# Attention scores as four 64x64 products at a time, two steps a visit, in a fused attention and MoE kernel

## The chip, the cores and the metric

The kernel runs on one core of one Trainium2 chip. The time is the device time of one execution in microseconds (us). Before the change the median of three runs is 390.88 us (390.87 to 391.03).

## The reference

```python
# q, k, v: (4 batches, 8 heads, 576 positions, 64 wide)
scores = q @ k^T / 8 - slope[h] * |rel|;  masked to 0 <= rel < 128
attn   = exp(scores - max) / sum
x      = (attn @ v) as (2304 tokens, 512)
# soft MoE: 8 experts, 4 slots each
logits = x @ phi
slots  = softmax_over_tokens(logits)^T @ x
slots  = relu(slots @ w1[e]) @ w2[e]
y      = softmax_over_slots(logits) @ slots
out    = relu(y @ w_in)^2 @ w_out        # 512 -> 2048 -> 512
```

## The kernel before

Everything is one program, in three stages: attention for 16 units (a unit `u` is a batch and a pair of heads), then the experts (H with w1, O with w2, lines 760 and 904), then the last layer (lines 957 and 1001), which is more than half of the time.

In attention a unit is cut into nine chunks `c` of 64 queries. A chunk needs at most 192 keys (itself and the two chunks before). The two heads share the 128 partitions: partitions 0 to 63 hold the 64 dimensions of the first head, 64 to 127 those of the second. One product per chunk gives the scores of both heads: its stationary side `zq` is a 128x128 block matrix, queries of head 0 in one corner, of head 1 in the other, zeros in the two others; its moving side `kq` is the keys, 128 partitions by 64, 128 or 192 columns. A float32 product is two passes through TensorE (PE), so the trace counts two MATMUL and two LDWEIGHTS per product.

A step `t` is two consecutive chunks: `emit_S` (line 180) does two products into one bank of PSUM (tag "S", three banks). Then, per chunk, `emit_max` on VectorE (DVE, line 193) adds the bias and takes the maximum, `emit_exp` on ScalarE (ACT, line 202) takes the exponential; `emit_sums`, `emit_fold` and `emit_norm` on GpSimd (POOL, lines 207 to 235) normalise; `emit_T` (PE, line 249) transposes; `emit_evac` (ACT line 269, DVE line 273) copies the transposes out; when all chunks of a unit are there, `emit_PV` (PE, line 285) multiplies by v, with weights of 64 columns, two heads on the two halves of the array's columns; `emit_xT` copies out (ACT). After that `emit_X` transposes (line 328), and for each batch `emit_logits` (line 315, weights of 32 columns, four on the array at once), `emit_logr` (line 321) and d0 to d4 keep a running softmax over tokens.

The order on every engine is fixed beforehand by `arrange`, a planner: each operation has an estimated duration, the operations it comes after, a due time and the PSUM banks that it takes; the planner gives out what can start first, by due time where two could. On SP, which issues the DMAs, it interleaves the loads of z and k of a unit (`load_z`, `load_k`, after the scores of the unit three earlier, whose buffer they take), of v (`load_v`, after the PV two earlier) and 38 half loads of 512 KB of expert weights (`load_half_w`, lines 82 and 88). Behind the attention, `load_extra` (line 97) loads five more expert tiles of 1 MB as the attention's buffers come free, then the first two tiles `f` of the last layer's weights and seven more tiles of w2 follow, then the other `f` (lines 70 and 74). A tile `f` is unpacked by POOL (line 813) and DVE (lines 826 to 830) before PE can use it.

Of the kernel before, what the change touches and what calls it, by code (L numbers as in the profile page):

```python
# [7 lines left out]
F32 = mybir.dt.float32  # L8
# [20 lines left out]
def attn_moe_relu2_kernel(ctx: ExitStack, tc: tile.TileContext, z, k, v, phi, w1, w2, w_in, w_out, bias, cst, out):  # L29
# [103 lines left out]
    zq = [zpool.tile([128, NCH, 2, 64], F32, name=f"zq{i}") for i in range(NQ)]  # L133
    kq = [zpool.tile([128, S], F32, name=f"kq{i}") for i in range(NQ)]
# [9 lines left out]
    kt_t, v_t, xT = {}, {}, {}  # L144
# [3 lines left out]
    zq.append(first[:, 0:2 * S].rearrange("p (c a b) -> p c a b", c=NCH, a=2))  # L148
    kq.append(first[:, 2 * S:3 * S])
# [250 lines left out]
    load_z(0, 0, 2)  # L400
    load_k(0, 0, 4, act)
    sp.dma_start(out=tbl[:, 0:192], in_=bias[:, 0:192])
    load_z(0, 2, 4, act)
    load_z(0, 4, 6)
    load_k(0, 4, 9, act)
    load_z(0, 6, 9)
    sp.dma_start(out=cs, in_=cst)
    sp.dma_start(out=tbl[:, 192:384], in_=bias[:, 192:384])
    load_z(1, 0, 3)
    load_k(1, 0, 3)  # L410
    load_z(1, 3)
    load_k(1, 3)
# [3 lines left out]
    load_k(2)  # L416
# [19 lines left out]
    STEP = 1450  # L436
# [5 lines left out]
    fin = {u: (NCH * u + NCH - 1) // 2 for u in range(NU)}  # L442
    alone = (0, 1)
    landed = {0: 0, 1: 900, 2: 2600, 3: 3500, 4: 5000, 6: 6000, 9: 10500}
    steps_of = lambda u: range(NCH * u // 2, fin[u] + 1)
    for u in range(1, NU):
        if u > 2:
            before = [x for y in range(u) if zslot(y) == zslot(u) for x in each(emit_S, *steps_of(y))]
            op(load_z, u, "SP", 1450, before, STEP * fin[u - 1] - 20000, (), 2300)
            op(load_k, u, "SP", 740, before, STEP * fin[u - 1] - 19990, (), 2300)  # L450
        op(load_v, u, "SP", 810, each(emit_PV, u - 2)[:u > 1], STEP * fin[u] - 6000, (), 2300)
    op(load_phi, 0, "SP", 200, (), 9000, (), 2300)
    for j in range(2 * RING):
        late = [u for u in range(NU) if zslot(u) == NQ + j // 2 - (RING - NZ)]
        late = late if j // 2 >= RING - NZ else []
        when = 15000 + 2400 * min(j, 31) + 1700 * max(0, j - 31)
        op(load_half_w, j, "SP", 1260, [x for u in late for x in each(emit_S, *steps_of(u))], when + 1000, at=when)
    for t in range(NS):
# [19 lines left out]
        op(emit_T, t, "PE", 222, each(emit_norm, *two), t0 + 3500, (("T", each(emit_evac, *two[:1 + bool(half)])),), 230)  # L478
        op(emit_evac, (t, 0), "ACT", 52 + 106 * len(full), each(emit_T, t) + free(full), t0 + 4000, (), 135)
        if half:  # L480
            op(emit_evac, (t, 1), "DVE", (0, 208, 342)[sum(x[1] > 1 for x in ch)] + 208 * sum(x[1] == 0 for x in ch), each(emit_T, t) + each(emit_evac, (t, 0)) + free(half), t0 + 4300, (), 120)
    for u in range(NU):
        b, kk = divmod(u, NPAIR)
        t0, odd, late = STEP * fin[u], b % 2, u == NU - 1
        parts = [(t, i) for t in range(NCH * u // 2, fin[u] + 1) for i in range(2) if (emit_evac, (t, i)) in ops]
        old = (each(emit_X, u - 4) + each(emit_logr, (u - 4) // NPAIR)) if 4 <= u < NU - 4 + 2 else []
        op(emit_PV, u, "PE", 1910, each(emit_evac, *parts) + each(load_v, u)[:u > 0], t0 + 5500, (("xa", each(emit_xT, u)), ("T" if late else "B", each(emit_xTb, u))), 190, 9500)
        op(emit_xT, u, "ACT", 477, each(emit_PV, u) + old, t0 + 7400, (), 165)
        op(emit_xTb, u, "DVE" if late else "ACT", 104, each(emit_PV, u) + old, t0 + 7450, (), 165)
# [708 lines left out]
```

## Time and profile before

| | us |
|---|---|
| median of three runs | 390.88 |
| the profiled execution's own time | 391.1 |
| its span, first to last instruction | 389.3 |
| PE busy | 381.8 |
| DVE busy | 274.6 |
| ACT busy | 243.9 |
| POOL busy | 117.4 |

Busy is the union of an engine's instructions in time; a PE that is busy need not work at its peak, since the ends of products are modelled. PEld is PE's loading of weights, which lies beside its products. The granted clock of TensorE is 1.0 of full speed in all 40 slices of the page. The chain that ended last runs through PE for 95% of the span.

### The profile page before, as it was taken

How to read it: one execution, taken by the hardware profiler on the slowest of the kernel's cores; microseconds unless marked ns; L12 is line 12 of the kernel's file. 1: busy time of each engine (PE TensorE's matmuls, PEld its weight loads, DVE VectorE, ACT ScalarE, POOL GpSimd, SP SyncE). 2: the span in 40 equal slices, each digit the busy share in tenths (PEclk: the TensorE clock that was granted, in tenths of full speed). 3: DMA queues.
4: the chain of work that ended last, by engine and by line, in shares of the span. 5: the costliest groups of instructions: out<-in, count | busy, mean ns of one | idle time of the engine just before them, and what ended most of it. 6: DMA issues, size and time to landing. Idle time of an engine off the chain costs nothing.

```text
span 389.3 us, 7986 instructions
## 1 busy us (share of the span) xinstructions
PE 381.8 (98%) x2654; PEld 300.2 (77%) x2654; DVE 274.6 (71%) x819; ACT 243.9 (63%) x728; POOL 117.4 (30%) x289
## 2 busy tenths in 40 slices
PE   8899999999999999999999999999999999999996
PEld 8798788788777346777877887888878888888884
DVE  5676786686775957578687888887767785466455
ACT  4989889789874220497776766766666644334440
POOL 4878678568660132131111102102100000000000
PEclk9999999999999999999999999999999999999999
DMA  7989999999978999998102200000000040012004
GB/s 227 339 257 389 411 400 380 387 340 411 397 266 319 416 427 421 417 422 356 43 2 108 109 2 0 0 2 0 0 3 1 0 164 0 2 52 110 2 1 162
DMA packets 23225, 75.36 MB, mean 194 GB/s; under 512 B 2832, under 2 KB 4624, under 8 KB 21520
## 3 DMA queue, kind: packets, MB, share of 16 engines
q1 hardware_dynamic: 22608, 74.30, 49.7%
q10 hardware_dynamic: 576, 0.56, 0.4%
q8 instruction: 21, 0.34, 0.4%
q14 instruction: 20, 0.16, 0.1%
HBM read 70.13 MB, written 4.72 MB: 192 GB/s over the span
## 4 chain that ended last, share of the span: by engine, by line
PE 95%; DVE 2%; POOL 1%; ACT 1%; DMA 1%; issue 0%; DVEq 0%; POOLq 0%; ACTq 0%
PE acc L1001 50%; PE s L184 11%; PE xa L285 7%; PE tp L249 5%; PE h L957 4%; PE H L760 4%; PE O L904 4%; PE X L328 2%; PE L L315 1%; PE MX L853 1%; DVE psum L1019 1%; PE xb L285 1%; DMA kq<-in_k_dram 1%; PE R L381 1%; POOL p L235 1%; PE L L321 1%
## 5 line engine op out<-in xcount | busy, mean ns | idle before, releaser
L1001 PE MATMUL acc<-whl,arena_gh 128*128 128x512 f32 x864 | 216.5, 394 | 0.0
L1001 PEld LDWEIGHTS acc<-whl,arena_gh 128*128 128x128 f32 x864 | 160.1, 188 | 35.3 <-issue 2.9
L986 DVE TENSOR_TENSOR arena_gh<-hT,arena_gh 128x384 fp32r<-128x384 f32 (+1 forms) x97 | 53.6, 553 | 30.1 <-ACT arena_gh L982 24.3
L202 ACT ACTIVATE p<-p,st 128x192 f32<-128x192 f32 (+1 forms) x144 | 61.4, 429 | 5.8 <-DVE st L193 5.1
L969 ACT ACTIVATE acc<-h 128x384 f32<-128x384 f32 x47 | 23.1, 493 | 64.9 <-PE h L957 64.9
L813 POOL TENSOR_SCALAR yw<-f 128x512 f32<-128x512 f32 x32 | 27.4, 862 | 99.2 <-DVE arena_cin L830 53.5
L235 POOL TENSOR_SCALAR p<-p,st 128x128 f32<-128x128 f32 (+1 forms) x142 | 49.8, 371 | 6.5 <-DVE st L212 5.1
L193 DVE CUSTOM_DVE_ANT_0 p<-s,tbl 128x192 f32<-128x192 f32 (+1 forms) x144 | 41.7, 325 | 10.4 <-PE s L184 10.2
L184 PE MATMUL s<-kq,zq 128*128 128x192 f32 (+2 forms) x198 | 39.3, 328 | 0.3 <-DMA kq<-in_k_dram 0.2
L957 PE MATMUL h<-cst_sb,Mst 128*128 128x384 f32 x95 | 32.2, 339 | 0.1
L184 PEld LDWEIGHTS s<-kq,zq 128*128 128x128 f32 x198 | 31.2, 199 | 1.0 <-DMA kq<-in_k_dram 0.5
L273 DVE TENSOR_SCALAR ptb<-tp 128x256 f32<-128x256 f32 (+1 forms) x64 | 24.1, 384 | 8.0 <-ACT ptb L269 7.8
L269 ACT ACTIVATE ptb<-tp 128x256 f32<-128x256 f32 (+1 forms) x72 | 25.2, 353 | 7.1 <-PE tp L249 6.5
L249 PE MATMUL tp<-cs,p 128*128 128x128 f32 x144 | 28.0, 281 | 1.5 <-POOL p L235 1.4
L227 POOL TENSOR_TENSOR p<-p 128x128 f32<-128x128 f32 (+1 forms) x63 | 26.8, 425 | 7.0 <-ACT p L202 4.3
L285 PE MATMUL xa<-ptb,vt 128*64 128x256 f32 (+1 forms) x256 | 27.8, 359 | 0.0
L202 ACT ACTIVATION_READ_ACCUMULATOR p<-p,st 128x1 f32 x144 | 27.4, 190 | 0.0
L978 DVE TENSOR_TENSOR hT<-acc 128x384 f32<-128x384 f32 x17 | 9.5, 557 | 23.3 <-ACT acc L969 23.2
L982 ACT ACTIVATE arena_gh<-hT 128x384 fp32r<-128x384 f32 x48 | 24.8, 516 | 0.7
L285 PEld LDWEIGHTS xa<-ptb,vt 128*64 128x64 f32 x256 | 16.9, 136 | 10.0 <-issue 2.8
L982 ACT ACTIVATE arena_gh<-acc 128x384 fp32r<-128x384 f32 x47 | 24.2, 515 | 0.6
L249 PEld LDWEIGHTS tp<-cs,p 128*128 128x128 f32 x144 | 18.3, 143 | 6.0 <-POOL p L235 3.8
(209 smaller groups left out, 483.6 us busy)
## 6 DMA issues: line engine op xcount, KB each, us to landing
w_w<-in_w_dram SPq DMA_DIRECT2D x38, 512.0 KB, 7.5
w_w<-in_w_dram SPq DMA_DIRECT2D x12, 1024.0 KB, 8.5
f<-in_w_in_dram SPq DMA_DIRECT2D x16, 512.0 KB, 9.9
f<-in_w_out_dram SPq DMA_DIRECT2D x16, 512.0 KB, 10.0
zq<-in_z_dram SPq DMA_DIRECT2D x9, 576.0 KB, 6.3
vt<-in_v_dram SPq DMA_DIRECT2D x16, 320.0 KB, 5.4
first<-in_z_dram SPq DMA_DIRECT2D x5, 576.0 KB, 5.8
out_dram<-psum SPq DMA_DIRECT2D x11, 256.0 KB, 2.0
```

The costliest lines, as they stand in the source:

```text
L184: pe.matmul(out=sb_t[t][:, 256 * i:256 * i + n], lhsT=zbuf(u)[:, c].rearrange("p a b -> p (a b)"), rhs=kt_t[u][:, 64 * c + 64 - n:64 * c + ...
L193: dve.tensor_tensor_reduce(out=p, in0=sb_t[t][:, 256 * i:256 * i + n], in1=tbl[:, 192 * pr + 192 - n:192 * pr + 192], scale=-0.125, scalar ...
L202: act.activation(out=p, in_=p, func=AF.Exp, bias=st[:, k + i:k + i + 1], scale=-1.0, accum_out=st[:, 4 + k + i:5 + k + i])
L227: eng.tensor_tensor(out=ap(True), in0=ap(True), in1=ap(False), op=ALU.subtract)
L235: eng.tensor_scalar(out=p, in0=p, scalar1=st[:, k + i:k + i + 1], scalar2=0.0, op0=ALU.mult, op1=ALU.add)
L249: pe.transpose(A[:, i, :], P[:, o:o + 128], ident)
L285: pe.matmul(out=out, lhsT=v_t[u][:, j, po:po + 64], rhs=pt[:, a:b, po:po + 64], start=(j == 0 or (j == 3 and a == 2)), stop=(j == 4 or (j ...
L813: pool.tensor_scalar(out=y.bitcast(F32), in0=t[:, a, :, 1].bitcast(F32), scalar1=2.0 ** -112, scalar2=0.0, op0=ALU.mult, op1=ALU.add)
L957: pe.matmul(out=hb[-1][:, 0:HB], lhsT=Mst[:, 128 * f:128 * f + 128], rhs=cst_sb[:, c0:c0 + HB], start=True, stop=True)
L982: act.activation(out=lo_t[i][1][hf][:, 0, cl], in_=rbuf[hf][:, cl], func=AF.Square)
L986: eng.tensor_tensor(out=gh[hf][:, 1, cl], in0=g[hf][:, cl], in1=gh[hf][:, 0, cl].bitcast(F32), op=ALU.subtract)
L1001: pe.matmul(out=acc_t[s], lhsT=gh[:, x, c0:c0 + 128], rhs=w[:, f % 2, y, :], start=(units[i] in firsts and a == 0), stop=(units[i] in last ...
```

## The change

The query matrix loses its zeros. Of a unit, `z` now holds three rows of 576 columns per partition: the queries, the keys, and the keys with the two heads in swapped order of partitions; it is the same number of bytes as z and k had together, and one load instead of two. In every second chunk the queries have the heads swapped, too. A chunk's scores are now two products of 64 rows by 64 columns of the array, one per head. A visit `w` of `emit_S` does two steps: it takes two banks, one per step, and per half `i` of the visit it issues four products, of two chunks that stand next to each other, on the four quarters of the array. A step's two chunks are now two apart (0 and 2, 1 and 3, ...). The planner's room for banks follows, and its due times and durations are other numbers.

```diff
-    def load_z(u, c0=0, c1=NCH, eng=sp):
-        eng.dma_start(out=zbuf(u)[:, c0:c1].rearrange("p c a b -> p (c a b)"), in_=z[u, :, 128 * c0:128 * c1])
-    def load_k(u, c0=0, c1=NCH, eng=sp):
-        kt_t[u] = kq[zslot(u)]
-        eng.dma_start(out=kt_t[u][:, 64 * c0:64 * c1], in_=k[u, :, 64 * c0:64 * c1])
+    def load_z(u, a=slice(0, 3), cl=slice(0, S), eng=sp):
+        eng.dma_start(out=zbuf(u)[:, a, cl], in_=z[u].rearrange("p (a s) -> p a s", a=3)[:, a, cl])
...
-    for g in range(2 * NS):
-        u, c = divmod(g, NCH)
...
+    for t in range(NS):
+        for i in range(2):
+            u, c = divmod(4 * (t // 2) + t % 2 + 2 * i, NCH)
...
-    def emit_S(t):
-        sb_t[t] = bank("S", "s")
+    def emit_S(w):
+        for t in (2 * w, 2 * w + 1):
+            sb_t[t] = bank("S", "s")
         for i in range(2):
-            u, c, n, e = info[2 * t + i]
-            pe.matmul(out=sb_t[t][:, 256 * i:256 * i + n], lhsT=zbuf(u)[:, c].rearrange("p a b -> p (a b)"),
-                      rhs=kt_t[u][:, 64 * c + 64 - n:64 * c + 64], start=True, stop=True)
+            for a in range(2):
+                u, c, n, e = info[2 * (2 * w + a) + i]
+                for r in range(2):
+                    h, rows = r ^ a, slice(64 * r, 64 * r + 64)
+                    pe.matmul(out=sb_t[2 * w + a][64 * h:64 * h + 64, 256 * i:256 * i + n], lhsT=zbuf(u)[rows, 0, 64 * c:64 * c + 64],
+                              rhs=zbuf(u)[rows, 1 + a, 64 * c + 64 - n:64 * c + 64], start=True, stop=True,
+                              tile_position=(64 * r, 64 * h), skip_group_check=True)
...
-    load_z(0, 0, 2)
-    load_k(0, 0, 4, act)
+    load_z(0, slice(0, 1), slice(0, 256))
+    load_z(0, slice(1, 3), slice(0, 256), act)
     sp.dma_start(out=tbl[:, 0:192], in_=bias[:, 0:192])
...
-            op(load_z, u, "SP", 1450, before, STEP * fin[u - 1] - 20000, (), 2300)
-            op(load_k, u, "SP", 740, before, STEP * fin[u - 1] - 19990, (), 2300)
+            op(load_z, u, "SP", 2190, before, STEP * fin[u - 1] - 20000, (), 2300)
...
-        op(emit_PV, u, "PE", 1910, each(emit_evac, *parts) + each(load_v, u)[:u > 0], t0 + 5500, ...
+        op(emit_PV, u, "PE", 1910, each(emit_evac, *parts) + each(load_v, u)[:u > 0], t0 + 3500, ...
...
-                if len(held[tag]) >= NBUF[tag]:
-                    for x in held[tag][len(held[tag]) - NBUF[tag]]:
...
+                n = len(held[tag]) - NBUF[tag] + sum(x[0] == tag for x in ops[k]["banks"][:i])
+                for x in held[tag][n] if n >= 0 else ():
...
```

How PE's row of work changes, first, where the scores of the units 2 (buffer `first`) and 3 (buffer `zq_92`) meet; `s` is a bank of scores, `tp` transposes of a step, `X` transposes of a unit's output, `xa` and `xb` the products with v. Before:

```order
L249 MATMUL tp<-cs,p_98 128x128 x2
L184 MATMUL s<-first 128x192 x2
L328 MATMUL X<-cs,xT_104 128x128 x4
L249 MATMUL tp<-cs,p_99 128x128 x2
L184 MATMUL s<-first 128x192
L184 MATMUL s<-kq_94,zq_92 128x64
L249 MATMUL tp<-cs,p_100 128x128 x2
L184 MATMUL s<-kq_94,zq_92 128x128
L184 MATMUL s<-kq_94,zq_92 128x192 x3
L285 MATMUL xa<-ptb,vt 64x256 x6
```

Now:

```order
L248 MATMUL tp<-cs,p_95 128x128 x2
L182 MATMUL s<-first 64x192 x6
L182 MATMUL s<-zq_92 64x64 x2
L248 MATMUL tp<-cs,p_96 128x128 x2
L248 MATMUL tp<-cs,p_97 128x128 x2
L327 MATMUL X<-cs,xT_102 128x128 x4
L182 MATMUL s<-zq_92 64x128 x2
L182 MATMUL s<-zq_92 64x192 x6
L248 MATMUL tp<-cs,p_98 128x128 x2
L248 MATMUL tp<-cs,p_99 128x128 x2
L182 MATMUL s<-zq_92 64x192 x8
L284 MATMUL xa<-ptb,vt 64x256 x6
```

Scores stand in blocks of eight products of half the weights' width, with whole transposes between, where before single steps of two products alternated with them. From the start of attention to the experts' first product, PE passes from one shape of weights to another 110 times, where it was 52.

Second, SP's row early in attention, where the first halves of expert weights (`w_w`) come: `first` and `zq_92` are the loads of the units 5 and 6. Before:

```order
L166 DMA vt<-in_v_dram 128x640
L88 DMA w_w_346<-in_w_dram 128x1024
L158 DMA first<-in_z_dram 128x1152
L162 DMA first<-in_k_dram 128x576
L82 DMA w_w_346<-in_w_dram 128x1024
L166 DMA vt<-in_v_dram 128x640
L88 DMA w_w_440<-in_w_dram 128x1024
L82 DMA w_w_440<-in_w_dram 128x1024
L158 DMA zq_92<-in_z_dram 128x1152
```

Now:

```order
L160 DMA vt<-in_v_dram 128x640
L156 DMA first<-in_z_dram 128x1728
L88 DMA w_w_414<-in_w_dram 128x1024
L82 DMA w_w_414<-in_w_dram 128x1024
L156 DMA zq_92<-in_z_dram 128x1728
L160 DMA vt<-in_v_dram 128x640
L88 DMA w_w_516<-in_w_dram 128x1024
L82 DMA w_w_516<-in_w_dram 128x1024
L88 DMA w_w_573<-in_w_dram 128x1024
```

The first half of weights moved behind unit 5's load, and two halves instead of four stand ahead of unit 6's. Ahead of the last unit's load there are 27 halves, where there were 29; the total of 38 is the same.

## Rows read from the trace of the kernel before

**Rows 1.** The page: PE's share, and the chain that ended last by engine and line.

```profile
PE 381.8 (98%) x2654; PEld 300.2 (77%) x2654; DVE 274.6 (71%) x819; ACT 243.9 (63%) x728; POOL 117.4 (30%) x289
...
PE 95%; DVE 2%; POOL 1%; ACT 1%; DMA 1%; issue 0%; DVEq 0%; POOLq 0%; ACTq 0%
PE acc L1001 50%; PE s L184 11%; PE xa L285 7%; PE tp L249 5%; PE h L957 4%; PE H L760 4%; PE O L904 4%; PE X L328 2%; PE L L315 1%; PE MX L853 1%; DVE psum L1019 1%; PE xb L285 1%; DMA kq<-in_k_dram 1%; PE R L381 1%; POOL p L235 1%; PE L L321 1%
```

**Rows 2.** Stretches: from:to and length, engines' busy us, granted clock, DMA share, GB/s.

```profile
0.00:18.00 18.00, 15.66 (x84) 13.51 (x86) 11.62 (x63) 11.68 (x48) 11.19 (x36) 1.00 0.88 291
18.00:26.00 8.00, 8.00 (x80) 7.02 (x77) 4.97 (x30) 7.27 (x30) 6.32 (x19) 1.00 0.71 198
26.00:80.00 54.00, 54.00 (x523) 44.68 (x521) 39.81 (x209) 46.79 (x198) 39.94 (x118) 1.00 1.02 391
80.00:88.00 8.00, 8.00 (x72) 6.69 (x72) 6.41 (x39) 7.48 (x35) 5.71 (x17) 1.00 0.94 331
88.00:106.00 18.00, 18.00 (x214) 15.02 (x211) 12.49 (x69) 16.95 (x73) 13.93 (x42) 1.00 1.03 406
106.00:122.00 16.00, 14.92 (x191) 12.07 (x189) 10.42 (x48) 9.65 (x38) 8.11 (x24) 1.00 0.78 266
122.00:157.00 35.00, 34.70 (x444) 16.84 (x445) 24.97 (x74) 7.95 (x20) 7.45 (x8) 1.00 1.01 420
```

**Rows 3.** The chain that ended last, in order of time: start us, us, what.

```profile
50.79 0.22 PE tp L249 x2
51.01 1.66 PE xa L285 x16
52.67 0.23 PE xb L285 x8
52.90 0.85 PE s L184 x4
53.75 0.22 PE tp L249 x2
53.97 0.65 PE s L184 x4
...
67.84 1.01 PE L L315 x32
```

**Rows 4.** Timeline of PE's weight loads: start us, us, what.

```profile
52.39 0.37 PEld L285 LDWEIGHTS xb<-ptb,vt 128*64 128x64 f32 x8
```

**Rows 5.** Stretches of 10 us, columns as in rows 2.

```profile
50.00:60.00 10.00, 10.00 (x94) 8.54 (x91) 7.75 (x46) 9.60 (x44) 8.11 (x25) 1.00 1.02 395
...
70.00:80.00 10.00, 10.00 (x82) 7.47 (x80) 7.25 (x38) 7.38 (x31) 5.61 (x17) 1.00 1.01 380
```

**Rows 6.** Groups of DVE by line and shape: busy us, mean ns, idle before.

```profile
L193 DVE CUSTOM_DVE_ANT_0 p<-s,tbl 128x192 f32<-128x192 f32 x112 | 36.1, 348 | 8.6 <-PE s L184 8.4 <-PE tp L249 0.2
```

**Rows 7.** Timeline of POOL and DVE where the third tile `f` arrives.

```profile
157.24 0.69 POOL L813 TENSOR_SCALAR yw<-f 128x512 f32<-128x512 f32 x1 [3.81 <-DMA f<-in_w_in_dram]
158.46 0.92 POOL L813 TENSOR_SCALAR yw<-f 128x512 f32<-128x512 f32 x1 [0.53 <-DMA f<-in_w_out_dram]
...
158.11 0.42 DVE L927 COPY dT<-O 128x256 f32<-128x256 f32 x1 [4.40 <-PE O L904]
158.45 0.42 DVE L826 TENSOR_SCALAR yw<-yw 128x512 int32<-128x512 int32 x1
159.45 0.42 DVE L721 COPY so<-X 128x256 f32<-128x256 f32 x1 [0.58 <-PE X L932]
```

**Rows 8.** Timeline of SP's queue: first half of weights, a z load, an extra.

```profile
19.37 1.24 SPq L88 DMA_DIRECT2D w_w<-in_w_dram  x1
...
21.86 0.33 SPq L158 DMA_DIRECT2D first<-in_z_dram  x1
...
112.95 9.93 SPq L97 DMA_DIRECT2D w_w<-in_w_dram  x5
```

**Rows 9.** Timeline of PE at the start.

```profile
3.77 2.50 PE L184 MATMUL s<-kq,zq 128*128 128x64 f32 x8 [0.21 <-DMA kq<-in_k_dram]
```

More of the change, by code (lines that the diff above doesn't have):

```diff
@@ L132, in attn_moe_relu2_kernel @@
     NZ = 1
-    zq = [zpool.tile([128, NCH, 2, 64], F32, name=f"zq{i}") for i in range(NQ)]
-    kq = [zpool.tile([128, S], F32, name=f"kq{i}") for i in range(NQ)]
+    zq = [zpool.tile([128, 3, S], F32, name=f"zq{i}") for i in range(NQ)]
     tbl = ppool.tile([128, 768], BF16, name="tbl")
@@ L456, in attn_moe_relu2_kernel @@
         when = 15000 + 2400 * min(j, 31) + 1700 * max(0, j - 31)
-        op(load_half_w, j, "SP", 1260, [x for u in late for x in each(emit_S, *steps_of(u))], when + 1000, at=when)
+        op(load_half_w, j, "SP", 1260, [x for u in late for x in each(emit_S, *visits(u))], when + 1000, at=when)
     for t in range(NS):
@@ L477, in attn_moe_relu2_kernel @@
         free = lambda l: each(emit_PV, *[owner[x] for x in l if owner[x] is not None])
-        op(emit_T, t, "PE", 222, each(emit_norm, *two), t0 + 3500, (("T", each(emit_evac, *two[:1 + bool(half)])),), 230)
+        op(emit_T, t, "PE", 222, each(emit_norm, *two), t0 + 4500, (("T", each(emit_evac, *two[:1 + bool(half)])),), 230)
         op(emit_evac, (t, 0), "ACT", 52 + 106 * len(full), each(emit_T, t) + free(full), t0 + 4000, (), 135)
         if half:
-            op(emit_evac, (t, 1), "DVE", (0, 208, 342)[sum(x[1] > 1 for x in ch)] + 208 * sum(x[1] == 0 for x in ch), each(emit_T, t) + each(emit_evac, (t, 0)) + free(half), t0 + 4300, (), 120)
+            op(emit_evac, (t, 1), "DVE", (0, 208, 342)[sum(x[1] > 1 for x in ch)] + 208 * sum(x[1] == 0 for x in ch), each(emit_T, t) + each(emit_evac, (t, 0)) + free(half), t0 + 300, (), 120)
     for u in range(NU):
@@ L484, in attn_moe_relu2_kernel @@
         t0, odd, late = STEP * fin[u], b % 2, u == NU - 1
-        parts = [(t, i) for t in range(NCH * u // 2, fin[u] + 1) for i in range(2) if (emit_evac, (t, i)) in ops]
+        parts = [(t, i) for t in range(NS) if any(x[0] == u for x in info[2 * t:2 * t + 2]) for i in range(2) if (emit_evac, (t, i)) in ops]
         old = (each(emit_X, u - 4) + each(emit_logr, (u - 4) // NPAIR)) if 4 <= u < NU - 4 + 2 else []
-        op(emit_PV, u, "PE", 1910, each(emit_evac, *parts) + each(load_v, u)[:u > 0], t0 + 5500, (("xa", each(emit_xT, u)), ("T" if late else "B", each(emit_xTb, u))), 190, 9500)
+        op(emit_PV, u, "PE", 1910, each(emit_evac, *parts) + each(load_v, u)[:u > 0], t0 + 3500, (("xa", each(emit_xT, u)), ("T" if late else "B", each(emit_xTb, u))), 190, 9500)
         op(emit_xT, u, "ACT", 477, each(emit_PV, u) + old, t0 + 7400, (), 165)
-        op(emit_xTb, u, "DVE" if late else "ACT", 104, each(emit_PV, u) + old, t0 + 7450, (), 165)
+        op(emit_xTb, u, "DVE" if late else "ACT", 104, each(emit_PV, u) + old, t0 + 9450, (), 165)
         if late:
@@ L527, in room @@
             when = 0
-            for tag, readers in ops[k]["banks"]:
-                if len(held[tag]) >= NBUF[tag]:
-                    for x in held[tag][len(held[tag]) - NBUF[tag]]:
-                        if x not in seen:
-                            return None
-                        when = max(when, seen[x])
+            for i, (tag, readers) in enumerate(ops[k]["banks"]):
+                n = len(held[tag]) - NBUF[tag] + sum(x[0] == tag for x in ops[k]["banks"][:i])
+                for x in held[tag][n] if n >= 0 else ():
+                    if x not in seen:
+                        return None
+                    when = max(when, seen[x])
             return when
```

84 lines of the change are left out of this document (41 added, 43 removed).

## The prediction

> **What bounds the kernel now.** I read the page first [rows 1]: PE is busy for 98% of the span and carries 95% of the chain that ended last; the scores, line 184, are 11% of that chain, 0.11 x 389.3 = 43 us. So a cheaper score product is cheaper on the path, until another engine is the bound. To find that engine I read stretches [rows 2]. From 18 to 106 us PE is busy in every us of 88. ACT is busy 7.27 + 46.79 + 7.48 + 16.95 = 78.5 of them, so it is 9.5 us from full. DVE and POOL are near 72%. The DMA engines stand at a share of 1.02 to 1.03 nearly throughout, which I take as full: there are holes at 18 to 26 (0.71), 80 to 88 (0.94) and 106 to 122 us (0.78), and none from 122 to 157 (1.01). So attention has PE at its limit, with ACT and the DMA engines close behind, and how near those two are decides this case as much as PE does.
>
> **The change part by part.**
>
> *Scores, the streams.* In the chain a step of two 192-column chunks is four passes in 0.65 us [rows 3], 0.163 us a pass, 0.325 us a product. A visit now has two halves of four products each. If the four quarters of the array work at once, a half costs one product's 0.325 us. There are 72 halves; in the 8 even units chunks 0 and 1 fall in one half, 128 columns at most, 0.217 us. Sum: 64 x 0.325 + 8 x 0.217 = 22.5 us in place of 43.
>
> Do quarters work at once? The trace shows it for columns only. In `xa` the two heads use the two halves of the array's columns: 12 passes of 256 and 4 of 128 columns would be 3.03 us one after another at 0.163 us per 192, and take 1.66 [rows 3]. In the logits four tiles of 32 columns do 32 passes of 128 columns in 1.01 us instead of 3.47 [rows 3]. Nothing in this trace has two tiles on different rows of the array. So the bounds: four at once 22.5 us; two at once 45 us. I take the first, since tiles by column reach 1.8 of 2 and 3.4 of 4, and the rows of a tile are only another side of the same array. In the sequence written, the four products of a half go to the four quarters, and the two that share columns write different banks.
>
> *Weight loads.* Before, four loads a step lie under four passes. Now a full visit has 16 loads of 64 columns. Eight loads of that width take 0.37 us in `xb` [rows 4], 0.046 us each; one after another 16 are 0.74 us, against 0.65 us of streams. So between nothing and 0.09 us x 32 visits = 2.9 us more. I take nothing, since loads (PEld, the second number of a stretch) lie beside products all through attention [rows 2], and keep 2.9 us for the range.
>
> *Changes of shape.* Around `xa` the trace shows what it costs to change the shape of the tiles. Going in: at two at once 3.03 / 2 = 1.52 us would do, and 1.66 are taken, 0.14. Coming out: the first scores behind take 0.85 us where others take 0.65, 0.20 [rows 3]. A pair is 0.34 us. In the order the changes grow from 52 to 110, 29 pairs more: 9.9 us. (At the 0.14 alone it would be 4 us.)
>
> *Sum on PE:* 43 - 22.5 - 9.9 = 10.6 us less work, out of 109 us from the first scores [rows 9] to the last at about 113; 7.7 with the loads in a row.
>
> *What is late next: ACT.* From 18 to 106 us PE's share of that gain is 10.6 x 88/109 = 8.6 us, and ACT would then have to do 78.5 us of work in 79.4. Its work is unchanged, and it depends on PE's transposes and DVE's maxima. In its full stretches of 10 us it reaches 9.60, in its poorest 7.38 [rows 5]. I take 95.5% all through: 78.5 / 0.955 = 82.2, a gain of 5.8 us. Ends: 0 (its waits go with the new order, not away) and 8.6.
>
> *Then the DMA engines.* The bytes are the same, with z, k and the swapped k in one load. If attention is shorter, its loads and the 38 halves of 512 KB must move in less time. What can be given back is idle time: (1.02 - 0.78) x 16 = 3.8 us in 106 to 122, and 0.08 x 8 = 0.6 in 80 to 88 [rows 2]: 4.5 us. The place where it bites is the third tile `f` of the last layer. POOL starts on it the moment it lands, 157.24 us, after 3.81 us of waiting; it is done at 157.93, DVE takes it at 158.45, and has 0.58 us of idle time before the copy of `so`, which PE needs [rows 7]. So there are 0.52 + 0.58 = 1.1 us to spare, and the end can move by 4.5 + 1.1 = 5.6 us before PE waits for a DMA there. SP's row takes something back: the first half of expert weights was issued at 19.37 us, ahead of unit 5's load at 21.86 [rows 8], and now stands behind it, with two halves instead of four ahead of unit 6's. Half a MB at 391 GB/s is 1.3 us; if that falls into the hole at 18 to 26, the cap is 4.3 us.
>
> *Start.* The first scores begin at 3.77 us, when the keys have landed [rows 9]; they now need 384 KB instead of 256. At 291 GB/s [rows 2] this is 0.45 us later, 0.9 if both issuing queues share alike. Against this stands that the second step's scores come in the same visit. ACT is busy only 11.68 of the first 18 us; I count nothing, plus or minus 0.9.
>
> *Banks.* A visit takes two of the three score banks, so its second bank is free only when both maxima of the visit before's first step are done, 0.35 us each [rows 6]; behind a visit that waits stand transposes and the product with v in PE's row, and ACT and POOL wait for those. Below, this cannot gain. Above, with both maxima exposed in each of 36 visits, it is 36 x 0.70 = 25 us. PE's other work (transposes, `xa`, `X`) is 109 - 43 = 66 us, 1.8 us between two visits on average, which covers two maxima; I take nothing here and keep it for the rivals.
>
> *The clock.* It is at 1.00 in every stretch, also where PE had 1.08 of 16 us idle [rows 2]; I expect no stretch with much more, so no cost; at half the clock PE's work in a stretch would take twice as long, which the order of work has no cover for.
>
> *Sum.* The gain is the smaller of ACT's 5.8 and the DMA engines' 5.6 to 4.3: I take 5.0. Of the profiled execution's 391.1 us (span 389.3 and 1.8 around it) 386.1 are left; the median stands 0.2 lower, so 385.9.
>
> **The rivals.**
>
> *Larger.* ACT fills to 99% and gives PE's whole 8.6, and the hole of 2.5 us at 18 to 26 us closes, too, which lifts the cap to 8.1: 7.5 less, 383.4. For it: PE alone has more to give than I count. Against it: SP's row there moves weights later, and 99% is more than any stretch shows.
>
> *Smaller.* Loads in a row, or bank waits of 0.15 us a visit (5.4 us in all), leave PE about 5 to 7 us, of which ACT's part and the dependence between the two engines take half: 2.5 less, 388.4. For it: DVE already waited 8.4 us for scores [rows 6]. Against it: the cover named above.
>
> *Nothing changes.* PE's gain comes back as waits of the same length. Against it: PE is the chain [rows 1].
>
> *Slower: the two row halves of a step don't run together.* Place: the two products of one chunk, which read different halves of the partitions and write the two halves of one bank. If only two of four quarters run at once, a half visit is 0.65 us, the streams are 45 us, and with 9.9 us for shapes PE has 11.9 us more than now, all on its chain; ACT and the DMA engines get slack and hide none of it: 402.8. It decides from the point where a half visit takes more than 43 - 9.9 = 33.1 us / 72 = 0.46 us. For it: no row shows tiles on two halves of the rows. Against it: the logits' four tiles write one bank at the same time [rows 3].
>
> The Trainium skill, TensorEngine Tiling (Array Packing), section Gotcha 1: PSUM Pressure, says that different row tiles write different banks and cannot use one bank at the same time. By the letter that is this rival: the two heads of a chunk are different row tiles, and share a bank. No row of this trace shows it; the logits' tiles differ by columns, so they don't test it. Read as a rule on one bank of the same partitions, it leaves the forecast alone, since the quarters that share partitions write different banks.
>
> **How the numbers follow.** Forecast 0.52 (its own range 384 to 388, from the caps 4.3 to 5.6, the start's 0.9 and ACT's reach), larger 0.12, smaller 0.18, nothing 0.04, slower by row halves 0.10, slower by bank waits over 0.29 us a visit (10.6 / 36) 0.04. A measurement of this kernel can tell about 0.2%, 0.8 us, from no change. Faster is 0.52 + 0.12 + 0.18 = 0.82, same 0.04, slower 0.14. The range goes from 381.5, the larger case with the start's 0.9 and another us in case more is spare at the third `f`, to 391.0, where the smaller case has shrunk to nothing; that leaves out the slower cases and little at the other end.
>
> **What would show it.** The streams: a full visit of 16 passes in about 0.65 us, near 1.0 with its changes of shape; 1.3 for the streams alone is the slower rival. Shapes: the first products behind a change 0.1 to 0.2 us longer than the next. ACT: 95% busy from 18 us to the last exponential; if it stays at 89% with attention shorter by nothing, banks or order are to blame. The DMA engines: no hole at 106 to 122 us any more, and POOL waiting for the third `f` with the copy of `so` behind it on the path; a hole that stays says that the cap was not reached. What would make the prediction wrong at once: PE waiting before visits for DVE's maxima, or PE idle in the expert stage for weights that came late by more than 1.1 us.

## The result, and the profile after

The changed kernel takes 387.44 us (median of 4 runs, 386.08 to 388.03), the kernel before beside it 390.95; the ratio is 0.9905, 95% interval 0.9878 to 0.9931. So it is faster by about 0.9%, 3.5 us, where 385.9 was forecast, with a range of 381.5 to 391.0. Line numbers of the changed kernel are 2 to 4 lower than before (the scores are L182, the product with v L284).

Its page, the part that answers to [rows 1]:

```profile
PE 373.7 (97%) x2942; PEld 277.7 (72%) x2942; DVE 273.4 (71%) x827; ACT 241.0 (62%) x728; POOL 117.7 (30%) x297
...
PE 88%; DMA 4%; DVE 3%; ACT 2%; POOL 1%; issue 1%; SPq 0%; DVEq 0%; ACTq 0%
PE acc L997 50%; PE s L182 6%; PE xa L284 6%; PE tp L248 5%; PE h L953 4%; PE H L756 4%; PE O L900 4%; DMA vt<-in_v_dram 3%; DMA zq<-in_z_dram 1%; PE X L327 1%; PE MX L849 1%; DVE psum L1015 1%; PE L L314 1%; PE xb L284 1%; ACT p L201 1%; POOL p L234 1%
```

The scores (`PE s`) fell from 11% to 6% of the chain that ended last. A load that was not on it stands there now with 3%: `vt<-in_v_dram`, the values of one unit.

The stretches of [rows 2] in the changed kernel (same columns):

```profile
18.00:26.00 8.00, 7.42 (x94) 4.93 (x92) 6.29 (x38) 7.82 (x35) 7.41 (x23) 1.00 0.84 282
26.00:80.00 54.00, 53.98 (x739) 37.40 (x735) 42.57 (x237) 51.10 (x224) 44.81 (x136) 1.00 1.02 410
...
106.00:122.00 16.00, 12.50 (x173) 9.05 (x173) 7.17 (x27) 5.48 (x17) 1.86 (x5) 0.89 0.80 288
122.00:157.00 35.00, 34.77 (x433) 17.27 (x433) 23.13 (x67) 6.31 (x14) 8.67 (x10) 1.00 1.01 421
```

ACT went from 46.79 to 51.10 of the 54 us from 26 to 80. The hole of the DMA engines at 18 to 26 us became smaller (0.84 after 0.71). The one at 106 to 122 us stayed (0.80 after 0.78), and in that stretch PE now idles for 3.5 us and its granted clock is 0.89.

The wait behind that, in the chain of the changed kernel (start us, us, what):

```profile
101.45 1.66 PE xa L284 x16
103.11 0.23 PE xb L284 x8
103.35 0.04 PE tp L248
103.39 9.74 DMA vt<-in_v_dram
```

and in PE's timeline, the products with v of the units 14 and 15:

```profile
106.56 1.74 PE L284 MATMUL xa<-ptb,vt 128*64 128x256 f32 x16
113.18 2.98 PE L284 MATMUL xa<-ptb,vt 128*64 128x256 f32 x16 [2.77 <-DMA vt<-in_v_dram]
```

PE waited for the last unit's values. They were issued at 103.39 us, when the product of unit 13 had freed one of the two buffers for values, and took 9.74 us. SP's timeline (issue us, us to issue) shows what stood ahead of them:

```profile
101.54 0.33 SPq L97 DMA_DIRECT2D w_w<-in_w_dram  x1
101.91 0.43 SPq L82 DMA_DIRECT2D w_w<-in_w_dram  x1
102.39 0.43 SPq L88 DMA_DIRECT2D w_w<-in_w_dram  x1
103.39 0.33 SPq L160 DMA_DIRECT2D vt<-in_v_dram  x1
```

That is an extra tile of 1 MB (L97) and two halves of 512 KB. In the kernel before, SP issued the last unit's values at 109.83 us, behind two halves but ahead of all five extra tiles; the same product started at 118.28 us, 4.11 us behind that of unit 14, and did not wait. That attention became shorter than the planner's times for these loads had it is how I read the new order; no run tests that.

Five marks in PE's timelines cut an execution into stages: the start of the product with v of the units 0, 14 and 15 (PV 0, 14, 15), the first product of the experts (H), and the end of the span. The experiments below are read by this table, all in us of the profiled execution:

| kernel | start to PV 0 | PV 0 to 14 | PV 14 to 15 | PV 15 to H | H to end | span |
|---|---|---|---|---|---|---|
| before | 16.99 | 97.18 | 4.11 | 8.66 | 262.4 | 389.3 |
| changed | 17.78 | 88.78 | 6.62 | 10.07 | 263.0 | 386.2 |
| changed, again (e0) | 17.97 | 88.70 | 6.59 | 8.66 | 263.0 | 384.9 |
| two quarters (e2) | 17.46 | 103.02 | 5.84 | 10.06 | 263.0 | 399.4 |
| full products (e3) | 18.54 | 97.13 | 5.32 | 8.66 | 263.0 | 392.6 |
| values first (e1) | 17.46 | 88.71 | 3.77 | 8.66 | 264.1 | 382.7 |
| values ahead of halves (e5) | 16.58 | 88.77 | 3.77 | 8.66 | 264.1 | 381.9 |
| copy on VectorE (e4) | 16.00 | 90.13 | 5.46 | 8.76 | 263.0 | 383.4 |
| z on two queues (e6) | 16.23 | 89.51 | 5.76 | 8.66 | 263.1 | 383.2 |
| e4 and e5 together (e7) | 17.36 | 90.11 | 3.78 | 8.75 | 264.7 | 384.7 |
| exponential halved (e8) | 17.07 | 87.68 | 6.10 | 8.65 | 263.1 | 382.6 |
| a round twice (e9) | 17.53 | 96.59 | 6.85 | 10.07 | 263.5 | 394.5 |
| values and z (e10) | 16.89 | 88.90 | 3.77 | 8.67 | 264.0 | 382.2 |

Attention from PV 0 to PV 14 is 8.4 us shorter. Of that, 0.8 is lost at the start, 2.5 in the wait for the values, 1.4 in what follows it at a lower clock, and 0.6 at the very end: PE's last product ended at 385.71 us before and at 382.01 now, 3.70 sooner, and 3.1 us of span are left. Why what follows that product takes 0.6 us longer is open. In four executions with the same order of work in it (changed, e0, e1, e5) the stretch PV 0 to 14 repeats within 0.1 us; the start does not (PV 0 at 16.0 to 18.0 us in the six profiles of kernels with the same start: the changed kernel, e0, e1, e5, and e4 and e7 below).

### The profile page after: what moved, and what is told of

Its sections match the earlier page's. It is cut to its first block, busy times and chain, and to the rows that moved or that the text cites. A ratio compares the mean times of both kernels' runs of the same rounds, so it can differ in the third digit from the quotient of the medians.

```text
span 386.2 us, 8627 instructions
## 1 busy us (share of the span) xinstructions
PE 373.7 (97%) x2942; PEld 277.7 (72%) x2942; DVE 273.4 (71%) x827; ACT 241.0 (62%) x728; POOL 117.7 (30%) x297
## 4 chain that ended last, share of the span: by engine, by line
PE 88%; DMA 4%; DVE 3%; ACT 2%; POOL 1%; issue 1%; SPq 0%; DVEq 0%; ACTq 0%
PE acc L997 50%; PE s L182 6%; PE xa L284 6%; PE tp L248 5%; PE h L953 4%; PE H L756 4%; PE O L900 4%; DMA vt<-in_v_dram 3%; DMA zq<-in_z_dram 1%; PE X L327 1%; PE MX L849 1%; DVE psum L1015 1%; PE L L314 1%; PE xb L284 1%; ACT p L201 1%; POOL p L234 1%
## 5 line engine op out<-in xcount | busy, mean ns | idle before, releaser
L201 ACT ACTIVATE p<-p,st 128x192 f32<-128x192 f32 (+2 forms) x144 | 61.4, 432 | 6.3 <-DVE st L192 6.0
L192 DVE CUSTOM_DVE_ANT_0 p<-s,tbl 128x192 f32<-128x192 f32 (+2 forms) x144 | 40.2, 324 | 6.3 <-PE s L182 5.3
L284 PE MATMUL xa<-ptb,vt 128*64 128x256 f32 (+1 forms) x256 | 29.0, 370 | 2.8 <-DMA vt<-in_v_dram 2.8
L248 PE MATMUL tp<-cs,p 128*128 128x128 f32 x144 | 29.0, 295 | 2.1 <-POOL p L234 1.2
L272 DVE TENSOR_SCALAR ptb<-tp 128x256 f32<-128x256 f32 (+1 forms) x72 | 25.0, 355 | 7.2 <-ACT ptb L268 7.0
L226 POOL TENSOR_TENSOR p<-p 128x128 f32<-128x128 f32 (+1 forms) x71 | 27.8, 395 | 5.2 <-ACT p L201 2.0
L284 PEld LDWEIGHTS xa<-ptb,vt 128*64 128x64 f32 x256 | 17.5, 140 | 13.9 <-issue 3.9
L268 ACT ACTIVATE ptb<-tp 128x256 f32<-128x256 f32 (+1 forms) x72 | 24.3, 352 | 3.7 <-PE tp L248 3.3
L182 PE MATMUL s<-zq 64*64 64x192 f32 (+2 forms) x396 | 24.2, 337 | 1.3 <-DMA zq<-in_z_dram 1.3
L248 PEld LDWEIGHTS tp<-cs,p 128*128 128x128 f32 x144 | 15.6, 141 | 13.2 <-POOL p L234 6.7
L965 ACT ACTIVATE hT<-h 128x384 f32<-128x384 f32 x48 | 22.7, 472 | 0.0
```

The costliest lines, as they stand in the source:

```text
L182: pe.matmul(out=sb_t[2 * w + a][64 * h:64 * h + 64, 256 * i:256 * i + n], lhsT=zbuf(u)[rows, 0, 64 * c:64 * c + 64], rhs=zbuf(u)[rows, 1 + ...
L192: dve.tensor_tensor_reduce(out=p, in0=sb_t[t][:, 256 * i:256 * i + n], in1=tbl[:, 192 * pr + 192 - n:192 * pr + 192], scale=-0.125, scalar ...
L201: act.activation(out=p, in_=p, func=AF.Exp, bias=st[:, k + i:k + i + 1], scale=-1.0, accum_out=st[:, 4 + k + i:5 + k + i])
L226: eng.tensor_tensor(out=ap(True), in0=ap(True), in1=ap(False), op=ALU.subtract)
L248: pe.transpose(A[:, i, :], P[:, o:o + 128], ident)
L284: pe.matmul(out=out, lhsT=v_t[u][:, j, po:po + 64], rhs=pt[:, a:b, po:po + 64], start=(j == 0 or (j == 3 and a == 2)), stop=(j == 4 or (j ...
```

## The experiments

All are edits of the changed kernel. The first four ran beside a kernel before of 390.81 us (9 runs), e4 to e7 beside 390.84 (13 runs), e8 to e10 beside 390.94 (9 runs).

### e0: the changed kernel again

> The changed kernel again, unchanged, on the chip of the runs beside it, so that they can be compared with it. Expected: 387.4 us, within 386 to 388, with the same wait of PE for the last unit's v (3 us) in its profile. If that wait is an accident of one execution, the profile shows none and the median is nearer 383.

386.72 us (385.3 to 387.33, 5 runs), ratio 0.9894 (0.9878 to 0.9909), within the expected 386 to 388. The wait is there again, but not the slow product behind it. First e0's timeline of PE:

```profile
106.67 1.73 PE L284 MATMUL xa<-ptb,vt 128*64 128x256 f32 x16
113.26 1.73 PE L284 MATMUL xa<-ptb,vt 128*64 128x256 f32 x16 [2.74 <-DMA vt<-in_v_dram]
```

Then two stretches of the execution shown above, the wait and what follows:

```profile
106.00:113.00 7.00, 3.75 (x54) 2.61 (x54) 2.60 (x9) 2.19 (x7) 1.86 (x5) 1.00 1.00 341
113.00:117.00 4.00, 3.82 (x46) 2.70 (x50) 0.38 (x3) 0.60 (x1) 0.00 (x0) 0.57 0.37 154
```

and the same two of e0:

```profile
106.00:113.00 7.00, 3.82 (x55) 2.61 (x54) 2.72 (x9) 2.30 (x8) 1.97 (x6) 1.00 0.96 337
113.00:117.00 4.00, 3.74 (x72) 3.00 (x73) 1.21 (x7) 0.63 (x2) 0.00 (x0) 1.00 0.50 195
```

PE was busy for 3.75 and 3.82 of the 7 us, so almost alike, and in one execution the granted clock of the next 4 us was then 0.57 (most of them at the lower of its two levels, 1.2 in place of 2.4 GHz), in the other 1.00. In the first the 16 passes took 2.98 us and not 1.73. So the wait costs 2.5 us in both, and the fall of the clock 1.4 more. The second execution is the exception: over the whole span the mean granted clock was 0.995 or 0.996 in all four runs of the changed kernel in the section above (0.996 in the one shown), and 0.988 to 0.995 in the four other runs of e0, where the kernel before has 0.998 or more. Where in those runs it fell no profile shows. Nor does the length of the wait alone decide: in e2 it was 2.00 us and the clock fell (the product took 2.69 us), in e8 2.25 us and it did not (1.73).

### e2: two quarters at a time

```diff
-                    h, rows = r ^ a, slice(64 * r, 64 * r + 64)
+                    h, rows = r, slice(64 * r, 64 * r + 64)
...
-                              rhs=zbuf(u)[rows, 1 + a, 64 * c + 64 - n:64 * c + 64], start=True, stop=True,
+                              rhs=zbuf(u)[rows, 1, 64 * c + 64 - n:64 * c + 64], start=True, stop=True,
...
-            if (u + c_) % 2:
+            if False:
```

The heads are never swapped, so all products go to the two quarters on the diagonal; number, shape and order of the products stay.

> The changed kernel with both heads' products on the two diagonal quarters of the array for both steps of a visit (queries in one order of heads only, keys from the first copy), so that only two of four products can run at once; same loads, same order, same number of products and of shape changes. Theory (four quarters run at once, which is where the gain comes from): a full visit's streams take 1.3 us and not 0.65, PE has 22.5 us more, attention is PE-bound again and 15 to 20 us longer: 400 to 407. Rival (products of one step share a bank and never ran together, so the changed kernel had two at once already): no change, 387 to 388.

401.15 us (400.02 to 401.29), ratio 1.0257 (1.0242 to 1.0273), slower, as the theory expected. A full visit in the chain of the changed kernel, and what stands around it:

```profile
52.12 0.23 PE xb L284 x8
52.36 0.37 PE tp L248 x2
52.72 0.70 PE s L182 x12
53.43 0.59 PE tp L248 x4
...
54.56 0.81 PE s L182 x16
55.37 0.37 PE tp L248 x2
```

and in e2's chain:

```profile
53.59 1.45 PE s L182 x16
55.04 0.59 PE tp L248 x4
```

0.81 us against 1.45 for the same 16 passes. At four passes in each 0.162 us a visit has 0.65 us of streams, at two passes 1.30; the rest, 0.16 and 0.15, I put down to the change of shape going in. So four quarters do work at once. The starts show it too, in a stretch of 0.06 us at the head of a visit, first of the changed kernel, then of e2:

```profile
54.49 0.39 PE L182 MATMUL s<-first 64*64 64x192 f32 x4
```

```profile
53.52 0.38 PE L182 MATMUL s<-zq 64*64 64x192 f32 x2
```

Four passes, one of each product, are under way at once in the one, two in the other. In e2 the first two products of a visit lie on different rows and write the two halves of one bank, and still start together; one after another, a visit would be 2.6 us. If only products on different banks could overlap, the order of e2's products would need five times 0.325 us for a visit in place of four, 1.62 us and more, and it takes 1.45. The Trainium skill, TensorEngine Tiling (Array Packing), section Gotcha 1: PSUM Pressure, says that different row tiles cannot use one bank at a time; for tiles that write different partitions of the bank these rows say otherwise.

### e3: full products in the new order

```diff
-                for r in range(2):
-                    h, rows = r ^ a, slice(64 * r, 64 * r + 64)
-                    pe.matmul(out=sb_t[2 * w + a][64 * h:64 * h + 64, 256 * i:256 * i + n], ...
+                q0 = max(0, 64 * c - 64)
+                pe.matmul(out=sb_t[2 * w + a][:, 256 * i:256 * i + n], lhsT=zbuf(u)[:, 0, q0:q0 + 128],
+                          rhs=zbuf(u)[:, 1, 64 * c + 64 - n:64 * c + 64], start=True, stop=True)
```

One 128x128 product per chunk, as before the change, in the order and with the loads of the changed kernel. Its scores are mixed between the two heads.

> The changed kernel with one 128x128 product per chunk in each visit, as before the change, in the changed kernel's order and with its loads; the scores come out mixed between the two heads, so the numbers of the result are not the reference's. It has 43 us of score streams and none of the 29 added pairs of shape changes (9.9 us). Theory (the quarters, not order or loads, bring the gain): PE has 10.6 us more than the changed kernel, attention is PE-bound as before, 390 to 395. Rival (the gain comes from the new order and from joining z and k into one load): 386 to 388.

394.05 us (393.6 to 394.43), ratio 1.0084 (1.007 to 1.0097), in the theory's range. Its chain:

```profile
52.40 0.37 PE tp L246 x2
52.77 1.30 PE s L181 x8
54.07 0.44 PE tp L246 x4
54.51 1.66 PE xa L282 x16
```

A visit takes 1.30 us, what two steps took before [rows 3]; the four transposes behind it take 0.44 where those behind quarters take 0.59. So a change out of the quarters costs 0.15 us, one in 0.16: 0.31 a pair. PV 0 to 14 takes 97.13 us, before 97.18. In that stretch the new order and loads alone give nothing in sum, and the 8.4 us come with the quarters. At the start and in the wait for the values e3 loses 1.6 and 1.2 us, which makes most of the 3.2 by which it is slower than before.

### e1: the last values first

```diff
+    seq = arrange()
+    iv = seq.index((load_v, NU - 1))
+    late = [x for x in seq[:iv] if x[0] is load_half_w][-2:]
+    seq = [x for x in seq[:iv + 1] if x not in late] + late + seq[iv + 1:]
...
+        if (f, a) == (load_v, NU - 1):
+            load_extra(owed[0])
```

The load of unit 15's values goes ahead of the extra tile and of the last two halves.

> The changed kernel with the last unit's load of v ahead, on SP, of the first extra expert tile (1 MB) and of the last two half loads issued before it (1 MB); nothing else moves. Theory (the gain of the shorter scores was there and is lost at the last unit's product with v, 3.0 us of PE waiting for v and 1.7 us of that product at half clock): PE waits for v less than 1 us, the clock stays 1.00 there, and the attention ends about 4.7 us earlier; of that 3.5 to 4.7 arrive at the end, so 382.7 to 384. Rival (the DMA engines bound the expert stage anyway, as in the prediction's cap): PE then waits for the third tile f or for w2 instead, and the time stays within 1 us of the changed kernel, 386.4 to 387.4.

384.62 us (384.1 to 384.83), ratio 0.9841 (0.9827 to 0.9854): above the theory's 382.7 to 384 and below the rival's 386.4, so each has a part. Its timeline of PE in the expert stage:

```profile
126.94 1.07 PE L763 MATMUL H<-yw,siT 128*32 128x512 f32 x8 [0.82 <-DMA yw<-in_w_dram]
```

The wait for the values is gone: PV 15 starts at 109.94 us, 3.3 us sooner than in e0. Of that, 1.1 is lost again: PE now waits 0.82 us in the expert stage for the tile `yw`. So a part of the cap that was forecast for the third `f` bites, 24 us earlier and at another tile.

### e5: the last values ahead of the halves only

```diff
+    late = [x for x in seq[:iv] if x[0] is load_half_w][-2:]
+    seq = [x for x in seq[:iv + 1] if x not in late] + late + seq[iv + 1:]
```

> Changed kernel with one difference: the load of the last unit's values goes ahead of the last two 512 KB half tiles, but stays behind the first extra 1 MB tile. Theory (in the changed kernel the last unit's PV waits for its values, because they queue behind 2 MB; with all of that moved behind them the DMA engines stood idle for 1.5 us at 102 to 104 us and the expert stage then waited 0.8 us for its tile yw): the extra tile fills that hole, the values still land before 109.9 us, so PV of the last unit does not wait, and the 0.8 to 1.0 us at yw come back too: 383.2 to 384.2 us. Rival (the values, issued at 103, still land only after 110 us since the 1 MB tile shares the engines with them): PV waits 0.5 to 2 us, 385 to 386.5 us.

385.11 us (383.69 to 385.62), ratio 0.9849 (0.9828 to 0.987); not told apart from e1. The hole of e1 at 102 to 104 us:

```profile
102.00:104.00 2.00, 1.61 (x23) 1.19 (x20) 0.70 (x5) 2.00 (x9) 1.83 (x7) 1.00 0.25 88
```

was filled in e5:

```profile
102.00:104.00 2.00, 1.62 (x17) 1.08 (x11) 1.53 (x8) 1.76 (x8) 1.83 (x7) 1.00 0.91 369
```

but e5's PE waits for `yw` as before:

```profile
126.26 1.07 PE L760 MATMUL H<-yw,siT 128*32 128x512 f32 x8 [0.95 <-DMA yw<-in_w_dram]
```

PV 15 starts at 109.12 us. From it to the product with `yw` it is 17.0 us in e1 and 17.1 in e5. The values are in time, as expected; that the hole is what `yw` lacks was wrong. What sets its landing stays open: it and the four extra tiles ahead of it are issued only when attention's memory comes free, and from then on the DMA engines have little idle time (their share in e1 is 1.00 to 1.02 from 110 to 126 us, in e5 0.95 to 1.00). No run moves either.

### e4 and e7: the copy of each product with v on VectorE

```diff
-        act.activation(out=xT[u][:, 0:512], in_=xa_t.pop(u), func=AF.Copy)
+        dve.tensor_copy(out=xT[u][:, 0:512], in_=xa_t.pop(u))
```

> Changed kernel with one difference: the copy of each unit's PV result (128x512, 16 times) runs on VectorE (0.69 us each) instead of ScalarE (0.58 us each); the order of all other work is the same. Theory (with the scores short, ScalarE bounds the attention, 94.7% busy between 26 and 80 us): ScalarE loses 9.3 us, so PV of unit 14 starts 2 to 6 us sooner than at 106.7, until VectorE (then some 90% busy) or TensorE ends last; the whole time falls less, by 0 to 2 us, since the last unit's values still arrive late: 384.7 to 386.7 us. Rival 1 (TensorE itself, or its order, bounds the attention): PV of unit 14 starts within 0.5 us of 106.7. Rival 2 (VectorE is as near its limit as ScalarE): it starts later, and the time is over 387 us.

387.29 us, ratio 0.9923 (0.9895 to 0.995), with 10 runs from 385.17 to 390.67, so of little weight for the whole time. The stretch PV 0 to 14 of the changed kernel, then of e4:

```profile
17.78:106.56 88.78, 87.25 (x1192) 60.17 (x1188) 70.64 (x390) 83.88 (x366) 74.21 (x224) 1.00 1.00 391
```

```profile
16.00:106.13 90.13, 87.95 (x1193) 59.97 (x1189) 78.20 (x403) 79.31 (x354) 74.25 (x224) 1.00 1.00 386
```

ACT lost 4.6 us of work there, DVE got 7.6, and the stretch became 1.4 us longer. That PV 14 starts at 106.13 is due to the start alone (PV 0 at 16.00). So taking work from ACT did not help, and the theory fell; but DVE's own work is in the way of a clean answer. e7, the same edit on e5:

> Changed kernel with two differences: the last unit's values loaded ahead of the last two half tiles, and the copy of each unit's PV result on VectorE. Theory (ScalarE bounds the attention, and what the attention gains after that is capped by the DMA engines, which are over 97% busy from 26 to 157 us but for a few holes): the attention ends 2 to 6 us sooner than with the earlier values alone, but the expert stage then waits for its tiles, and of that gain no more than 1 us reaches the end: 382.3 to 384 us. Rival (the DMA engines still have room): 1.5 to 4 us reach the end: 379 to 382 us.

386.64 us (385.56 to 386.96), ratio 0.9889 (0.9874 to 0.9905), above both expectations and 1.5 us above e5: attention did not end sooner, so it could not tell how much the DMA engines would let through. It repeats e4's finding.

### e8: half of the exponential

```diff
-        p = pbuf[t % NP][:, e:e + n]
+        p = pbuf[t % NP][:, e:e + n // 2]
         act.activation(out=p, in_=p, func=AF.Exp, ...
```

> Changed kernel, with ScalarE's exponential over the left half of each chunk's score columns only (the other half stays without it); no other instruction changes or moves. It takes work from ScalarE and gives none to another engine, as moving the PV copies to VectorE did not. From the start of PV of unit 0 to that of unit 14 the changed kernel took 88.7 to 88.8 us in four profiles. Theory 1 (ScalarE, 94.7% busy, bounds this stretch): 144 exponentials each 0.08 to 0.15 us shorter, 12 to 20 us off ScalarE; the stretch shortens by 2 to 8 us until another engine ends last. Theory 2 (the chain TensorE, VectorE, POOL in its fixed order bounds it, and ScalarE only fills): the stretch stays within 0.7 us of 88.75.

Half of the scores are left without their exponential. 384.39 us in one run. Its stretch PV 0 to 14:

```profile
17.07:104.75 87.68, 86.81 (x1192) 60.05 (x1188) 70.12 (x389) 77.61 (x366) 74.05 (x223) 1.00 1.00 394
```

ACT has 6.3 us less to do here (12 to 20 were expected over all units; it is busy for 88.5% in place of 94.5%), and the stretch shortens by 1.1. PE's idle time falls from 1.53 to 0.87 us. This lies between the two theories and much nearer to the second: ACT holds attention back by about 1 us.

### e9: a round of products twice

```diff
-        for i in range(2):
+        for i in (0, 0, 1):
```

> Changed kernel, with the first half of each visit's score products issued twice (the same values are written again): two more rounds of four quarters, 0.325 us more of TensorE in each of 36 visits, 11.7 us in all and some 10.7 us between PV of unit 0 and PV of unit 14. With two quarters instead of four, 0.64 us a visit, that stretch grew from 88.75 to 103.0 us, 14.3 us for some 21 us added. Theory 1 (TensorE has slack behind ScalarE, some 7 us): the stretch grows by 2 to 5 us. Theory 2 (TensorE's chain bounds it all the way): it grows by 9 to 11 us.

396.29 us in one run. Its stretch PV 0 to 14:

```profile
17.53:114.12 96.59, 95.60 (x1432) 68.79 (x1428) 72.14 (x389) 85.23 (x364) 74.41 (x223) 1.00 0.97 356
```

The stretch grew by 7.8 us, between the theories again and nearer to the second. What PE was given there is shown by the scores' own share of the same stretches, in the changed kernel, e9 and e2 (stretch, length, PE's and PEld's busy us on scores, granted clock, DMA share, GB/s):

```profile
17.78:106.56 88.78, 25.59 (x484) 15.35 (x480) 1.00 1.00 391
```

```profile
17.53:114.12 96.59, 34.87 (x724) 24.06 (x720) 1.00 0.97 356
```

```profile
17.46:120.48 103.02, 41.50 (x482) 28.92 (x480) 1.00 0.93 335
```

PE's time on scores grew by 9.3 us in e9 and by 15.9 in e2 (22.5 were expected there over all units, as if every half visit took twice as long), and the stretch by 7.8 and 14.2. So 84 and 90% of what PE was given arrive at PV 14: PE's row is the bound of attention in the changed kernel too, as its 87.25 busy us of 88.78 say, with a slack of some 1.5 us.

### e6: unit 0's queries and keys on two queues

```diff
+    load_z(0, slice(1, 3), slice(256, S), act)
+    load_z(0, slice(0, 1), slice(256, S))
     sp.dma_start(out=tbl[:, 0:192], in_=bias[:, 0:192])
-    load_z(0, cl=slice(256, S))
```

> Changed kernel with one difference: the second part of unit 0's queries and keys is issued in two pieces, two thirds on ScalarE's queue right behind the first part, one third on SyncE's ahead of the bias. In the changed kernel the second visit of the scores waits till 7.28 us for it, and ScalarE, the bound of the attention, has done only 3.1 us of work in the first 8 us. Theory (the start is late by the landing of that load, and the bound carries it to the end of attention): the second visit starts at 5.5 to 6.7 us, PV of unit 14 0.5 to 1.5 us sooner; the whole time falls by 0 to 1 us. Rival (the load is limited by the DMA engines and not by where it stands): the second visit starts within 0.3 us of 7.28 and nothing moves.

386.19 us (385.01 to 387.69), ratio 0.9895 (0.9873 to 0.9918), not told apart from e0. The changed kernel's start:

```profile
4.11 1.34 PE L182 MATMUL s<-zq 64*64 64x64 f32 x16 [0.55 <-DMA zq<-in_z_dram]
7.34 1.65 PE L182 MATMUL s<-zq 64*64 64x192 f32 x16 [0.74 <-DMA zq<-in_z_dram]
```

and e6's:

```profile
4.00 1.07 PE L182 MATMUL s<-zq 64*64 64x64 f32 x16 [0.45 <-DMA zq<-in_z_dram]
5.64 0.54 PE L182 MATMUL s<-zq 64*64 64x192 f32 x4
6.49 0.87 PE L182 MATMUL s<-zq 64*64 64x192 f32 x12 [0.31 <-DVE st L192]
...
9.18 0.76 PE L182 MATMUL s<-zq 64*64 64x192 f32 x16
11.09 0.99 PE L182 MATMUL s<-zq 64*64 64x192 f32 x16 [0.78 <-DMA zq<-in_z_dram]
```

The second visit comes 1.7 us sooner, as the theory had it, but stands still behind its first four passes until DVE's maxima of the first visit are done (0.31 us), since its second bank is free only then; the third comes only 1.2 us sooner (10.39 in the changed kernel) and a later one waits for the next load. PV 0 is early (16.23), the stretch PV 0 to 14 is 0.7 us longer than in the changed kernel (89.51), and PV 14 starts at 105.74, within the spread that kernels with the old start show (105.35 to 106.67).

### e10: values ahead of the halves, and z on two queues

This is e5 and e6 together.

> Changed kernel with the last unit's values ahead of the last two half tiles, and with the second part of unit 0's queries and keys in two pieces on two queues. Theory (the time after the attention is held by the DMA engines, so an earlier start gives little, but the start no longer depends on when one load lands, 6.8 or 7.3 us): 384 to 385 us, with the runs within 1 us of each other. Rival (the start is worth what PV of unit 0 gains, 0.4 to 1.7 us): 383.3 to 384 us. If the runs still lie 2 us apart, the spread is not from that load.

384.01 us (383.4 to 384.21, 5 runs), ratio 0.9818 (0.9804 to 0.9831). That lies where the theory's range (384 to 385) meets the rival's (383.3 to 384), so it doesn't decide between them; the runs are 0.8 us apart, as the theory had it. It is the fastest kernel here, 1.8% under before and some 3 us under the changed kernel; from e1 it is not told apart for certain (the intervals overlap). The wait for `yw` is still in it.

## Why the prediction was right, step by step

*Scores.* Right. Four quarters work at once; a full visit takes 0.81 us, of which 0.65 are its streams. The rival of the row halves (402.8) is what e2 made of the kernel by giving up two quarters, 401.15.

*Weight loads.* Right. The 16 loads of a visit take 0.53 us beside the products, in the changed kernel's timeline of PEld:

```profile
100.57 0.53 PEld L182 LDWEIGHTS s<-zq 64*64 64x64 f32 x16
```

*Changes of shape.* 0.34 us a pair was forecast, 0.31 measured on full visits.

*PE's sum.* 10.6 us were forecast for all 576 passes of scores; 484 of them lie between PV 0 and PV 14, for which that makes 8.9. The stretch gave 8.4, and 9.5 with ACT eased (e8).

*ACT as the next bound.* This step failed. "I take 95.5% all through" made 5.8 us of PE's 8.6. ACT's share did rise to 94.5%, since it has the same work in a shorter stretch, but ACT was not the bound: e8 returned 1.1 us of ACT's 6.3, while e9 and e2 passed on 84 and 90% of what PE was given. What ACT takes off PE's gain should have been about 1 us and was put at 8.6 - 5.8 = 2.8.

*The DMA engines' cap.* It was there, in the wrong place. By PV 14 the changed kernel is 7.6 us ahead (106.56 for 114.17), more than the cap of 5.6. The first load to come late was not the third `f` but the last unit's values, which the text did not name; they took 2.5 us, and 1.4 more where the clock fell behind them. The third `f` still has nearly the time to spare that [rows 7] showed, in the changed kernel's timelines of POOL and DVE:

```profile
153.72 0.68 POOL L809 TENSOR_SCALAR yw<-f 128x512 f32<-128x512 f32 x1 [3.98 <-DMA f<-in_w_in_dram]
...
154.76 0.42 DVE L822 TENSOR_SCALAR yw<-yw 128x512 int32<-128x512 int32 x1
155.76 0.42 DVE L717 COPY so<-X 128x256 f32<-128x256 f32 x1 [0.58 <-PE X L928]
```

0.36 us from POOL's end to DVE, 0.58 idle ahead of the copy: 0.94 of 1.1. The hole at 106 to 122 us stayed, which was named as the sign that the cap was not reached there. Only with the values in time (e1, e5, e7, e10) does a tile of the expert stage come late.

*Start.* Nothing, plus or minus 0.9, was forecast; 0.8 was lost in the profiled execution, and other executions lie from 1.0 above to 1.0 below the one profiled execution of the kernel before.

*Banks.* Right from 18 to 106 us: no wait of PE for DVE's maxima stands among its waits there.

*Clock.* "No stretch with much more" idle time was wrong, since the wait for the values made one, and in the profiled execution the lower clock behind it cost 1.4 us.

So the forecast's first half, cheaper scores on PE's path, was right, and its second half, the two caps that made 5.0 us of it, was not what acted. That the sum came out near, 3.5 us against 5.0, is luck: two errors are of opposite sign. By PV 14 the kernel was 7.6 us ahead and not 5.0, and 3.9 went at a load that the prediction does not name.

## What to carry to other kernels

An engine that rises to 95% busy when another gets faster is not thereby the next bound; take work from it and see what returns, and do so without giving the work to a third engine. What an experiment gives an engine is read from the trace, not from the plan. When a stage gets shorter, list every load that waits for a buffer to come free late in that stage, and what is queued ahead of it: its issue comes sooner by the stage's gain, but the bytes ahead of it do not. Cutting the span at a few fixed instructions told a gain of 8.4 us, repeated within 0.1 in four executions, from a start that varies by more than 1 us.

## What the runs showed of the hardware

Tiles of 64x64 on all four quarters run at once, also two that lie on different rows and write different partitions of one bank: 0.81 us for a visit against 1.45 on two quarters. A visit takes 0.16 us more than its streams where PE goes into such tiles, and the four transposes behind it 0.15 more than behind full products (0.59 and 0.44). After almost the same idle time (3.75 and 3.82 of 7 us busy) the granted clock of the next 4 us was 0.57 in one execution and 1.00 in another. A load of 320 KB took 9.74 us from issue to landing with about 2 MB issued in the 2 us ahead of it, and 2.7 us in e1, where these 2 MB stood behind it.
